# Loading v of the first batch once, in the layout of the later products, and turning eight units on TensorE in 128 by 32 tiles

## The chip, the cores and the metric

The kernel runs on one core of one Trainium2 chip. A core has five engines that matter here: TensorE (PE; its weight loads are listed as PEld), VectorE (DVE), ScalarE (ACT), GpSimd (POOL) and SyncE (SP), which here does nothing but issue DMAs. The metric is the device time of one execution in microseconds (us); a kernel's time is the median of its runs.

## What is computed

```python
# attention: q, k, v are (8 batches, 8 heads, 576 rows, 64), float32
scores = scale * np.matmul(q, k.transpose(0, 1, 3, 2))
thresh = np.max(scores, axis=-1, keepdims=True) - tau
scores = np.where(scores >= thresh, scores, -1000000000.0)
scores = scores - np.max(scores, axis=-1, keepdims=True)
attn = np.exp(scores)
attn = attn / (np.sum(attn, axis=-1, keepdims=True) + 1e-09)
attn_out = np.matmul(attn, v)
# rows: (batch, head, row, 64) -> x of 4608 x 512
# feed-forward: w_a, w_b are 512 x 1536, w_out 1536 x 512, given as float64
a = x @ w_a
b = x @ w_b
out = a * b @ w_out
```

## The kernel before

Heads are worked on in pairs: `pairs` holds 32 of them (8 batches, HP = 4 pairs each), and a tile's 128 partitions hold two heads of 64. A unit `(i, u)` is 128 query rows of pair i (u = 0 to 3), or the last 64 rows of two pairs together (u = NT). The main loop goes over the units, one slot g for each. Slot g computes the scores of unit g (line 404), their maximum (L411), the exponentials (L432) and the threshold with the sums (L435), and then has the weights of earlier units turned, so that the 576 keys lie on partitions, and multiplied by v (L546, output `pv`). Between these steps `advance` emits portions of the feed-forward block (L854, L750, L920 and L990), in amounts worked out when the program is built. `keep_order` fixes the order of the instructions on each engine to the order in which they are emitted.

The weights of a unit are turned in one of two ways.

- The first BY_PE = 8 units (u = 0 and 1 of the four pairs of the first batch) are turned by TensorE in `turn_pe`, one slot later. `diagonals` (L462) makes a diagonal matrix `dg` of the reciprocal sums; a matmul with 64 columns of the weights `tw` as the stationary operand and `dg` as the moving one (L483) gives these 64 keys by 128 rows, transposed and normalised, in PSUM. There are NSLOT = 9 slots of 64 keys and two heads j, so 18 such matmuls a unit, each in a 128 by 64 tile of the array. Two ScalarE copies (L485) and one VectorE copy (L486) take them to `wT`. `weighted_unit` multiplies by v one slot after that.
- All later units are turned by `normalise` (L454), a VectorE transpose of 32 by 32 blocks (L502) and a trip through DRAM: `turn_blocks` writes `swap`, `turn_back` reads it into `wT`.

The two ways leave the keys in different places. With TensorE, slot s and partition p (of 64) hold key 64 s + p. With the block transpose, partition c 32 + p and slot s hold a key of half c, block s, place p: 288 c + 32 s + p for the first batch. The rows of v have to lie in the same way in the tile `vm`, whose partitions are two heads of 64.

`load_v` therefore loads v of the first four pairs twice. The first load, from SyncE (L214), is two moves of 144 KB a pair in the layout of `turn_pe`. It is emitted ahead of the loop for pair 0, and at the end of slots 0, 1 and 2 for pairs 1 to 3. The second load, `again=True`, is four moves of 72 KB a pair in the layout of the block transpose, into the same tile. It is emitted at the end of slots 8 to 11 through `post`, which at that time issues at once on SyncE (L144). The products of units u = 2, 3 and NT of the first batch (L546 and L629) read what it brings.

In the same stretch of slots the float64 weights are brought in and turned into float32: 36 pieces, loaded by `load_weights` on SyncE (L271), at most one at each of five places of a slot, some of them held back until an instruction of TensorE has run. ScalarE (L298, L299), GpSimd (L305, L324) and VectorE (L311, L319) convert them, two or three pieces a slot.

SyncE issues its DMAs strictly in the order emitted. DMA number n of the queue waits, by the program's semaphores, for number n - 8.

Of the kernel before, what the change touches and what calls it, by code (L numbers as in the profile page):

```python
# [10 lines left out]
FP32 = mybir.dt.float32  # L11
# [12 lines left out]
BY_PE = 8  # L24
# [30 lines left out]
def kernel(  # L55
# [38 lines left out]
    nc = tc.nc  # L94
    B, H, S, D = q.shape
    P = 128
    Q = 32
    DM = H * D
    DFF = w_a.shape[1]
    HP = H // 2  # L100
    NT = 4
# [10 lines left out]
    NSLOT = 9  # L112
# [5 lines left out]
    def pool(name, bufs, **kw):  # L118
        return ctx.enter_context(tc.tile_pool(name=name, bufs=bufs, **kw))

    const = pool("const", 1)
    loads = pool("loads", 3)
# [5 lines left out]
    def banks(n, name):  # L128

        return psum.tile([P, 2, 512], FP32, tag="banks", name=name)[:, :, 0:n]  # L130
# [4 lines left out]
    loaded = {}  # L135
# [3 lines left out]
    def post(key, *moves):  # L139

        if not state["paced"]:
            for move in moves:
                state["turn"] += state["over"]
                (nc.scalar if state["turn"] % 2 else nc.sync).dma_start(*move)  # L144
        else:
            at = len(bulk)
            if key[0] in ("tw", "wT"):
                while at and bulk[at - 1][0][0] not in ("tw", "wT") and bulk[at - 1][1] >= state["slot"] - 1:
                    at -= 1
            bulk.insert(at, (key, state["slot"], moves))  # L150
# [47 lines left out]
            engine.dma_start(room[:, :, j * D:(j + 1) * D], rows.rearrange("(n p) d -> p n d", p=R))  # L198
        loaded.setdefault(i, {})[name] = room

    def load_v(i, again=False):
        b, hp = pairs[i]
        if not again:
            loaded[i]["v"] = loads.tile([P, NSLOT, D], FP32, tag="vm", bufs=HP, name="vm")
        for j in range(2):
            rows, half = v[b, 2 * hp + j], loaded[i]["v"][j * D:(j + 1) * D]
            if i >= HP or again:
                if i < HP:
                    rows = rows.rearrange("(c s p) d -> p c s d", c=2, p=Q)
                else:  # L210
                    rows = rows.rearrange("(p c s) d -> p c s d", c=2, p=Q)
                post(("v", i), *((half[c * Q:(c + 1) * Q], rows[:, c]) for c in range(2)))
            else:
                nc.sync.dma_start(half, rows.rearrange("(s p) d -> p s d", p=D))  # L214

# [8 lines left out]
    for f in range(NG):  # L226
        for c in range(HP):
            for dst, w in ((wa_sb, w_a), (wb_sb, w_b)):
                src = []
                for r in range(2):  # L230
                    chunks = [(2 * c + e) % HP * 2 + (r + (c >= HP // 2)) % 2 for e in range(2)]
                    cols = slice(f * CW + r * CH, f * CW + (r + 1) * CH)
                    rows = w[:, cols].bitcast(U32).rearrange("(k p) f -> p k f", p=D)
# [110 lines left out]
    load_rows(2, "k", rooms[5])  # L344
    load_weights(RAWS)
    load_v(0)
    load_rows(3, "q", rooms[6])
    load_rows(3, "k", rooms[7])
# [19 lines left out]
    def prep_pe(i, name):  # L368

        m = loaded[i][name]  # L370
        if name == "q":
            mT = first_sb[:, i * S:(i + 1) * S]
        else:
            mT = work.tile([P, S], FP32, tag="kT", bufs=HP, name="kT")
        tp = banks(SH, "tp")
        for c in range(2):
            for n in range(NR // 2):
                nc.tensor.transpose(tp[:, c, n * R:(n + 1) * R], m[:, c * (NR // 2) + n], ident[0:R, 0:R])
        prepared.setdefault(i, {})[name] = mT
        return mT, tp  # L380
# [86 lines left out]
    def turned_tile(here=None):  # L467
        if here == (0, NT):
            return sums_sb[:, NSUM - TURNED:].rearrange("p (g s e) -> p g s e", g=G + 1, s=NSLOT)
        return work.tile([P, G + 1, NSLOT, Q], FP32, tag="wT", bufs=2, name="wT")  # L470

    def turn_pe(i, u):

        ws, dg = weights.pop((i, u))
        ws = [w.rearrange("p n e -> p (n e)") for w in ws]
        wT = turned_tile()[:, 0:G].rearrange("p g s e -> p (g s e)").rearrange("p (s w) -> p s w", w=P)
        turned[i, u, "pe"] = [wT[:, :, y * D:(y + 1) * D] for y in range(2)]
        tp = banks(512, "tp").rearrange("p y (s q) -> p y s q", s=NT)
        last = banks(P, "tp")
        for s in range(NSLOT):  # L480
            for j, w in enumerate(ws):
                to = (last[:, 0] if s == 2 * NT else tp[:, s // NT, s % NT])[j * D:(j + 1) * D]
                nc.tensor.matmul(to, w[:, s * D:(s + 1) * D], dg[:, j], start=True, stop=True)  # L483
        for y in range(2):
            nc.scalar.copy(wT[:, y * NT:(y + 1) * NT], tp[:, y])  # L485
        nc.vector.tensor_copy(wT[:, 2 * NT], last[:, 0])  # L486
# [524 lines left out]
    def store(n):  # L1011

        for _ in range(n):
            post("out", pending.pop(0))
# [79 lines left out]
    kT, tp = prep_pe(0, "k")  # L1094
# [22 lines left out]
    for g in range(len(units) + PV_LAG):  # L1117
# [14 lines left out]
        if here:  # L1132
            i, u = units[g]
# [33 lines left out]
        if g < 3:  # L1167
            kT, tp = prep_pe(g + 1, "k")
            nc.scalar.copy(kT.rearrange("p (c k) -> p c k", c=2), tp)
        if 0 < g <= BY_PE:  # L1170
            turn_pe(*units[g - 1])
# [42 lines left out]
        for p in range(1, NPR):  # L1214
            if g == first[p] - 1:
                load_v(p)
        if BY_PE <= g < BY_PE + HP:
            load_v(g - BY_PE, again=True)
        store(written)
        if g > BY_PE:  # L1220
            if held:
# [60 lines left out]
```

## Time and profile before

| what | us |
|---|---|
| median of 3 runs | 1401.8 |
| the three runs | 1399.14, 1401.8, 1404.3 |
| the profiled execution, its own time | 1400.57 |
| its span on the core | 1398.8 |

| engine | busy us | share of the span |
|---|---|---|
| PE | 1361.5 | 97% |
| PEld | 1258.5 | 90% |
| DVE | 1013.9 | 72% |
| ACT | 680.8 | 49% |
| POOL | 492.8 | 35% |

The profile is one execution recorded by the hardware profiler. Busy time is an average over stages with different limits, so the first 200 us have to be looked at by themselves. A matmul of float32 leaves two records: the 144 turning instructions of L483 stand as 288. A tile given as 128*64 is a tile of the array with 128 rows and 64 columns. DMA issues appear as SPq; the time of such a line can contain the issue's own wait. The DMA share is the mean busy share of the 16 DMA engines; in the busiest stretches it reads above 1.

Lines that the change touches, from the groups and the tiles of the trace:

| line | what | count | one takes |
|---|---|---|---|
| L483 | PE, 128*64, 128 columns | 288 | 272 to 475 ns |
| L485 | ACT, `wT` from PSUM, 128x512 | 16 | 1.07 us for two |
| L214 | SPq, first load of v, 144 KB | 8 | 595 to 638 ns |
| L144 | SPq, second load of v, 72 KB | 16 | 447 to 1587 ns, median 453 |

### The profile page before, as it was taken

How to read it: one execution, taken by the hardware profiler on the slowest of the kernel's cores; microseconds unless marked ns; L12 is line 12 of the kernel's file. 1: busy time of each engine (PE TensorE's matmuls, PEld its weight loads, DVE VectorE, ACT ScalarE, POOL GpSimd, SP SyncE). 2: the span in 40 equal slices, each digit the busy share in tenths (PEclk: the TensorE clock that was granted, in tenths of full speed). 3: DMA queues.
4: the chain of work that ended last, by engine and by line, in shares of the span. 5: the costliest groups of instructions: out<-in, count | busy, mean ns of one | idle time of the engine just before them, and what ended most of it. 6: DMA issues, size and time to landing. Idle time of an engine off the chain costs nothing.

```text
span 1398.8 us, 76307 instructions
## 1 busy us (share of the span) xinstructions
PE 1361.5 (97%) x33836; PEld 1258.5 (90%) x33836; DVE 1013.9 (72%) x2205; ACT 680.8 (49%) x1248; POOL 492.8 (35%) x675
## 2 busy tenths in 40 slices
PE   7889999999999999999999999999999999999998
PEld 5677588999998799999999999998899998799998
DVE  6999877787777768786767776778777776745425
ACT  6977555545554555544454545454545455431110
POOL 2764543424150607060515142332515060708100
PEclk9999999999999999999999999999999999999999
DMA  9977876667666775676556775566656775550000
GB/s 211 241 212 223 204 206 173 174 170 187 174 154 168 190 192 155 176 190 160 143 143 160 186 180 159 136 190 169 181 130 161 199 190 154 137 146 19 4 19 18
DMA packets 327449, 223.21 MB, mean 160 GB/s; under 512 B 171600, under 2 KB 311632, under 8 KB 327120
## 3 DMA queue, kind: packets, MB, share of 16 engines
q1 hardware_dynamic: 323936, 216.95, 60.1%
q8 instruction: 266, 4.36, 1.3%
q10 hardware_dynamic: 3184, 1.38, 0.4%
q14 instruction: 63, 0.52, 0.1%
HBM read 128.58 MB, written 89.65 MB: 156 GB/s over the span
## 4 chain that ended last, share of the span: by engine, by line
PE 88%; DMA 5%; DVE 4%; SPq 2%; issue 1%; ACT 1%; ACTq 0%; DVEq 0%
PE pab L750 29%; PE po L920 22%; PE pab L854 18%; PE sc L404 9%; PE pv L546 9%; SPq L144 1%; DMA vm<-in_v_dram 1%; DMA wT<-swap 1%; DVE tw L435 1%; DVE mx L411 1%; DMA more_u<-in_moe_w_a_dram 1%; DVE low L311 0%; DMA more_u<-in_moe_w_b_dram 0%; DVE tw L502 0%; DMA sums_u<-in_k_dram 0%
## 5 line engine op out<-in xcount | busy, mean ns | idle before, releaser
L454 ACT ACTIVATE tw<-tw,rcp 128x576 f32<-128x576 f32 x272 | 196.1, 768 | 201.3 <-DVE rcp L448 201.3
L411 DVE TENSOR_REDUCE mx<-sc 128x1 f32<-128x576 f32 x288 | 204.6, 752 | 121.2 <-PE sc L404 120.9
L432 ACT ACTIVATE tw<-sc,bias,scalars 128x576 f32<-128x576 f32 x288 | 239.6, 832 | 10.4 <-DMA qT<-in_q_dram 0.4
L712 POOL TENSOR_TENSOR h<-h,u 128x512 f32<-128x512 f32 x28 | 35.2, 1277 | 590.4 <-DVE h L824 414.1
L435 DVE SCALAR_TENSOR_TENSOR tw<-sc,thr,tw 128x576 f32<-128x576 f32 x288 | 220.9, 797 | 12.3 <-ACT tw L432 11.9
L920 PE MATMUL po<-wo_sb,h 64*64 64x256 f32 (+1 forms) x3408 | 210.5, 367 | 0.0
L502 DVE STREAM_TRANSPOSE tw<-tw 128x576 f32<-128x576 f32 x272 | 194.4, 752 | 0.8 <-ACT tw L454 0.8
L920 PEld LDWEIGHTS po<-wo_sb,h 64*64 64x64 f32 x3408 | 169.8, 133 | 14.9
L404 PE MATMUL sc<-kT,qT 64*64 64x288 f32 x2016 | 170.3, 404 | 1.8 <-issue 0.9
L546 PE MATMUL pv<-wT,vm 64*64 64x128 f32 (+2 forms) x4896 | 164.0, 275 | 3.7 <-DMA vm<-in_v_dram 1.4
L546 PEld LDWEIGHTS pv<-wT,vm 64*64 64x64 f32 x4896 | 153.2, 133 | 12.0 <-issue 4.0
L920 PE MATMUL po<-sums_u,h 64*64 64x256 f32 x2448 | 156.6, 376 | 0.0
L883 POOL TENSOR_TENSOR h<-h 128x256 f32<-128x256 f32 x168 | 117.2, 731 | 110.9 <-PE po L920 106.1
L750 PE MATMUL pab<-xU,wb_sb 64*64 64x128 f32 x4352 | 137.8, 269 | 0.0
L920 PEld LDWEIGHTS po<-sums_u,h 64*64 64x64 f32 x2448 | 126.1, 133 | 12.3 <-DVE h L862 0.5
L750 PEld LDWEIGHTS pab<-xU,wb_sb 64*64 64x64 f32 x4352 | 133.3, 133 | 1.8 <-ACT h L806 0.5
L404 PEld LDWEIGHTS sc<-kT,qT 64*64 64x64 f32 x2016 | 108.8, 133 | 17.3 <-issue 4.9
L431 ACT ACTIVATE bias<-mx,scalars 128x1 f32<-128x1 f32 x288 | 82.7, 287 | 66.1 <-DVE mx L411 65.6
L553 ACT COPY xT<-pv 128x128 f32<-128x128 f32 (+1 forms) x68 | 17.6, 259 | 193.5 <-PE pv L546 193.5
L750 PE MATMUL pab<-xS,wa_sb 64*64 64x128 f32 x2176 | 108.5, 269 | 0.8 <-issue 0.8
L554 DVE COPY xT<-pv 64x128 f32<-64x128 f32 (+1 forms) x136 | 38.1, 280 | 80.5 <-PE pv L546 79.0
L535 ACT COPY kept<-po 128x512 f32<-128x512 f32 x65 | 34.8, 535 | 120.3 <-PE po L920 106.4
(163 smaller groups left out, 2468.7 us busy)
## 6 DMA issues: line engine op xcount, KB each, us to landing
wT<-swap SPq DMA_DIRECT2D x242, 288.0 KB, 3.8
swap<-tw SPq DMA_DIRECT2D x480, 144.0 KB, 3.1
vm<-in_v_dram SPq DMA_DIRECT2D x128, 72.0 KB, 2.6
swap<-tw SPq DMA_DIRECT2D x128, 72.0 KB, 2.9
kT<-in_k_dram SPq DMA_DIRECT2D x112, 72.0 KB, 3.2
wT<-swap SPq DMA_DIRECT2D x56, 144.0 KB, 3.6
out_dram<-kept SPq DMA_DIRECT2D x27, 256.0 KB, 3.7
qT<-in_q_dram SPq DMA_DIRECT2D x112, 40.0 KB, 2.8
```

The costliest lines, as they stand in the source:

```text
L404: nc.tensor.matmul(sc[m][o * D:o * D + wide, c], qT[r, q0:q0 + wide], kT[r, c * SH:(c + 1) * SH], start=True, stop=True)
L411: nc.vector.tensor_reduce(mx[:, c], sc[j], axis=AX.XY, op=ALU.max)
L431: nc.scalar.activation(bias[:, j:j + 1], mx[:, j:j + 1], AF.Copy, scale=e_nscale)
L432: nc.scalar.activation(wb[j], sb[j], AF.Exp, bias=bias[:, j:j + 1], scale=e_scale)
L435: nc.vector.scalar_tensor_tensor(out=wv, in0=sb[j], scalar=thr[:, j:j + 1], in1=wv, op0=ALU.is_ge, op1=ALU.mult, accum_out=sums[:, j:j + 1])
L454: nc.scalar.activation(w, w, AF.Copy, scale=rcp[:, j:j + 1])
L502: nc.vector.transpose(w, w)
L546: nc.tensor.matmul(pv[c * D:(c + 1) * D, y], vm[rows, s], wT[y](rows, s), start=(s == 0), stop=(s == NSLOT - 1))
L750: nc.tensor.matmul(out[c * D:(c + 1) * D, r, f * P:(f + 1) * P], w[g][k][rows, w0:w0 + D], moving[k][rows], start=(fresh and k == 0 and f ...
L854: nc.tensor.matmul(pab[c:c + columns(), r], w[rows, f // n, k, fs + c:fs + c + columns()], moving, start=(k == 0), stop=(k == H - 1))
L883: (nc.vector if state["over"] else nc.gpsimd).tensor_tensor(*a, **kw)
L920: nc.tensor.matmul(po[c * D:(c + 1) * D, r, y, cut], ht[rows, t0:t0 + D], other[rows, f, cut], start=(f == 0), stop=(f == NF // 2 - 1))
```

## The change

v of the first batch is loaded once, in the layout that only the second load had: four moves of 72 KB a pair from SyncE, at the places of the first load. The second load goes. To fit, `turn_pe` puts keys of both halves c into each slot: instead of 64 neighbouring columns of the weights it takes two groups of 32, one from each half of the 576 keys, each by a matmul of its own whose output goes to 32 partitions. A unit has 36 such matmuls in 128 by 32 tiles instead of 18 in 128 by 64 tiles, each with the same 128 moving columns. The copies out of PSUM and the order of all other instructions stay as they were.

```diff
-    def load_v(i, again=False):
+    def load_v(i):
         b, hp = pairs[i]
-        if not again:
-            loaded[i]["v"] = loads.tile([P, NSLOT, D], FP32, tag="vm", bufs=HP, name="vm")
+        loaded[i]["v"] = loads.tile([P, NSLOT, D], FP32, tag="vm", bufs=HP, name="vm")
         for j in range(2):
             rows, half = v[b, 2 * hp + j], loaded[i]["v"][j * D:(j + 1) * D]
-            if i >= HP or again:
-                if i < HP:
-                    rows = rows.rearrange("(c s p) d -> p c s d", c=2, p=Q)
-                else:
-                    rows = rows.rearrange("(p c s) d -> p c s d", c=2, p=Q)
-                post(("v", i), *((half[c * Q:(c + 1) * Q], rows[:, c]) for c in range(2)))
+            if i < HP:
+                rows = rows.rearrange("(c s p) d -> p c s d", c=2, p=Q)
             else:
-                nc.sync.dma_start(half, rows.rearrange("(s p) d -> p s d", p=D))
+                rows = rows.rearrange("(p c s) d -> p c s d", c=2, p=Q)
+            moves = [(half[c * Q:(c + 1) * Q], rows[:, c]) for c in range(2)]
+            if i < HP:
+                for move in moves:
+                    nc.sync.dma_start(*move)
+            else:
+                post(("v", i), *moves)
...
         for s in range(NSLOT):
-            for j, w in enumerate(ws):
-                to = (last[:, 0] if s == 2 * NT else tp[:, s // NT, s % NT])[j * D:(j + 1) * D]
-                nc.tensor.matmul(to, w[:, s * D:(s + 1) * D], dg[:, j], start=True, stop=True)
+            for c in range(2):
+                for j, w in enumerate(ws):
+                    at = j * D + c * Q
+                    to = (last[:, 0] if s == 2 * NT else tp[:, s // NT, s % NT])[at:at + Q]
+                    k0 = (c * NSLOT + s) * Q
+                    nc.tensor.matmul(to, w[:, k0:k0 + Q], dg[:, j], start=True, stop=True)
...
-        if BY_PE <= g < BY_PE + HP:
-            load_v(g - BY_PE, again=True)
```

## The prediction

> **What bounds the kernel now.** I read the page's first part, then busy time by stage, then the chain of waits, then the TensorE and SyncE timelines of the stages that the edit touches.
>
> The columns of the first fence are: stretch and its length, then for PE, PEld, DVE, ACT and POOL the busy time (instructions), granted clock, DMA share, GB/s.
>
> ```profile
> 20.00:40.00 20.00, 17.30 (x326) 14.05 (x326) 17.02 (x44) 16.27 (x35) 11.40 (x15) 1.00 1.17 222
> 40.00:85.00 45.00, 36.48 (x796) 32.31 (x786) 42.34 (x90) 38.81 (x80) 34.86 (x41) 0.96 0.88 215
> 85.00:125.00 40.00, 35.41 (x583) 31.93 (x577) 39.21 (x85) 31.72 (x64) 22.27 (x23) 1.00 0.87 253
> 125.00:200.00 75.00, 72.31 (x1165) 51.95 (x1165) 66.91 (x144) 44.71 (x84) 39.77 (x30) 1.00 0.80 204
> 200.00:1398.00 1198.00, 1187.62 (x30943) 1118.78 (x30934) 839.14 (x1824) 539.17 (x970) 382.02 (x559) 1.00 0.57 150
> ```
>
> There are three regimes. Until 40 us the 16 DMA engines are full (share 1.17). From 40 to 125 us VectorE is the bound: it is busy 42.34 of 45 and 39.21 of 40 us, while TensorE has idle time (8.5 and 4.6 us). From 200 us TensorE is busy 99% and sets the end. Everything that the change touches lies before 125 us, so it can reach the end only by moving the moment at which that first part is through. The amount of work that TensorE does inside it is fixed by the emitted order.
>
> The chain of waits, by line, names two things that the change removes or alters:
>
> ```profile
> PE pab L750 29%; PE po L920 22%; PE pab L854 18%; PE sc L404 9%; PE pv L546 9%; SPq L144 1%; DMA vm<-in_v_dram 1%; DMA wT<-swap 1%; DVE tw L435 1%; DVE mx L411 1%; DMA more_u<-in_moe_w_a_dram 1%; DVE low L311 0%; DMA more_u<-in_moe_w_b_dram 0%; DVE tw L502 0%; DMA sums_u<-in_k_dram 0%
> ```
>
> The vm share (about 14 us) looks large. In order of time the chain's longest vm step is 8.52 us at 30.77, one of the first loads waiting in a full queue; the steps of the second load are 3.14 and 2.86 us at 92 and 102 us, and VectorE worked without a gap beside both.
>
> The TensorE timeline shows one turn of today's form (line 483), the product that waits for v behind it, and a later product of 128 columns; idle time and its cause stand in brackets.
>
> ```profile
> 27.89 2.19 PE L483 MATMUL tp<-first_u,tw 128*64 128x128 f32 x36
> 30.00 1.53 PE L404 MATMUL sc<-kT,first_u 64*128 64x288 f32 x8
> 31.98 0.33 PE L546 MATMUL pv<-wT,vm 64*64 64x64 f32 x4 [0.45 <-DMA vm<-in_v_dram]
> 32.87 1.26 PE L546 MATMUL pv<-wT,vm 64*64 64x64 f32 x68 [0.56 <-DMA vm<-in_v_dram]
> ...
> 113.27 2.20 PE L546 MATMUL pv<-wT,vm 64*64 64x128 f32 x72
> ```
>
> A unit's 18 turning instructions leave 36 records ("passes"). 36 passes in 2.19 us, less the last one's own length (0.27), is 1.92, or 53.3 ns a pass. A single pass lasts 273 ns, so several overlap. That two column halves run side by side, 107 ns of streaming each, is the reading that also fits the product: its 72 passes of 128 columns over four 64x64 tiles take 2.20 us, 107/4 = 27 ns each.
>
> **The change part by part.**
>
> *Turning in 128x32 tiles.* 18 instructions a unit become 36, so 72 passes of 128 columns each, for eight units; the two ScalarE copies and the VectorE copy behind them do not change, nor does the last slot's wait for its bank. No row has a 128x32 tile. Lower bound: four tiles of 107 ns side by side give 72 x 26.7 = 1.92 us, as today; a gain is excluded, because each quarter of the array still streams 128 columns 18 times. Upper bounds: two at a time, 72 x 53.3 = 3.84 us (+1.92 a unit, +15.4 in all); one at a time, 72 x 107 = 7.7 us (+5.8 a unit, +46 in all). The nearest row is the product of four 64x64 tiles, 72 passes in 2.20 us against 2.19 now. Today's two column halves already stream different data side by side at no loss, so I take 0.
>
> The Trainium skill ("TensorE: Matmul & The Clock Gate", section "Measured speedup vs the span model") speaks against taking the full overlap: three column tiles of 32 ran 2.38 times as fast as one after the other, and no four of them stand there. By that rule, as an estimate, a pass would cost 107/2.38 = 45 ns and a unit 3.2 us, +10.5 us of TensorE time in all, which is still below the 11.2 us of idle time worked out under the rivals. No run so far shows such a tile.
>
> *First load of v.* Two moves of 144 KB a pair become four of 72 KB, same bytes, same rows of 256 B. On SyncE the 144 KB move takes 0.606 us (median of 8) and the 72 KB one 0.45 (median of the 16 reloads): 4 x 0.45 - 2 x 0.606 = +0.6 us a pair, +2.4 us for four. Behind them in SyncE's queue stand the rows of pair 3 (first case) and then the weight pieces. The work that hides this is the DMA backlog: these moves land 7 to 8 us after issue, with the DMA share above 1, so a later issue meets a shorter queue. If the cover failed it would be the whole 2.4 us. Each move also waits for the eighth before it, so four small ones among eight leave 4 x 72 + 4 x 256 = 1.3 MB in flight, 6 us at 222 GB/s, still no gap. What may show is v itself: the product already waits 1.4 us for it, three times, and the fourth move ends 0.6 us later. I take +0.5; bounds 0 and 2.4.
>
> *Reload removed.* Sixteen moves of 72 KB go, and with them their time on SyncE:
>
> ```profile
> 83.32 3.08 SPq L144 DMA_DIRECT2D vm<-in_v_dram  x4
> 86.56 0.35 SPq L271 DMA_DIRECT2D more_u<-in_moe_w_out_dram  x1
> ...
> 90.93 3.19 SPq L144 DMA_DIRECT2D vm<-in_v_dram  x4
> 94.17 0.97 SPq L144 DMA_DIRECT2D wT<-swap  x2
> ...
> 101.06 1.94 SPq L144 DMA_DIRECT2D vm<-in_v_dram  x4
> ...
> 112.27 1.95 SPq L144 DMA_DIRECT2D vm<-in_v_dram  x4
> ```
>
> That is 10.2 us of SyncE and 1.18 MB (4.7 us at 253 GB/s). Queued behind them are w_out pieces and reads of swap. No product waits for the reload: the two that follow it, at 113 and 120 us, start with no idle time before them. VectorE has 0.8 us of idle time in the whole stretch, so w_out pieces that come sooner are converted no sooner. Bounds: 0 and, if all idle time of TensorE from 85 to 200 us (4.6 + 2.7) were owed to this queue, -7.3. I take -0.4, half of VectorE's idle time.
>
> *Sum*: 0 + 0.5 - 0.4 = +0.1 us on the profiled execution's 1400.6 (span 1398.8, 1.8 around it). The median shown is 1401.8, 1.2 above it; on that median the forecast is 1402, no change. What a measurement can tell from no change is about 0.5%, 7 us: below 1394.8 is faster, above 1408.8 slower.
>
> **Rivals.**
>
> *Column tiles one after the other (slower).* Place: TensorE, eight turns between 18 and 77 us. Idle time of TensorE that can swallow it: 2.7 + 8.5 = 11.2 us from 20 to 85. One at a time costs 46 - 11 = +35 us, 1437. It passes +7 when eight times (72s - 1.92) exceeds 18, that is from a spacing s of 58 ns a pass. Two at a time (53 ns) therefore costs only +4, 1406. The cover is uneven, which makes it dearer: the turn at 58.44 ended at 60.68 and VectorE took its result at 61.24, and the scores at 63.39 ended 0.2 us before VectorE needed them. Against: today's halves overlap without loss. For: no row has four full-height streams.
>
> *Second load was the brake (faster).* If SyncE's 10.2 us did hold the w_out pieces and swap reads, the end comes up to 7.3 us earlier, 1395. For: the chain names vm and SyncE. Against: VectorE's 39.21 of 40, and the absent idle time before the products.
>
> *The clock (either sign).* From 75 to 85 us the granted clock is 0.83, after TensorE idled 1.45 us before 78.36; the two groups after it took 2.08 and 1.81 us where others take 1.16 and 1.09, and VectorE then waited 1.43 us for scores. Denser turning could avoid this (-1.6) or longer waits add another such stretch (+1.6): 1400 or 1404.
>
> **How the numbers follow.** No change, including two at a time and the clock: 0.54, of which two tiles at a time 0.12. Slower: 0.32, namely one at a time or nearly 0.15, between 58 and 80 ns a pass, or two at a time where the uneven cover fails, 0.12, first loads that starve the weight pieces in the DMA-bound part 0.05. Faster: 0.14, the brake together with the clock. The predicted time is that of the likeliest case, 1402, whose own range is 1398 to 1406. The range goes down to 1395 for the brake and up to 1418: two at a time at full price with no cover, 1401.8 + 15.4. The serial case, 1437, lies outside it.
>
> **What would show it.** Turning line: 72 records in about 2.2 us a unit if I am right, 3.8 or 7.7 if not. First v moves: landing within 1 us of before, idle time of the product for vm at most 3 us. From 85 to 125 us: SyncE 10 us emptier, VectorE again about 98% busy; if its work there ends over 3 us sooner, the reload was the brake. From 200 us on both traces should agree. A granted clock that differs from 18 to 85 us, or a weight piece waited for where none was, would make the prediction wrong.

## The result, and the profile after

| | median us | runs | lowest to highest |
|---|---|---|---|
| before | 1403.01 | 17 | 1397.06 to 1405.34 |
| after | 1408.27 | 17 | 1402.62 to 1414.54 |

The ratio is 1.0038, with a 95% interval from 1.0023 to 1.0053: the changed kernel is 5.3 us slower. That is less than the 7 us set as "no change" beforehand, but the interval leaves out 1. The profiled execution took 1410.14 us, its span 1408.3.

Busy time by stage of the kernel after, up to 125 us, with the same columns as in the prediction:

```profile
20.00:40.00 20.00, 15.50 (x359) 12.23 (x348) 15.69 (x41) 14.72 (x31) 10.26 (x14) 0.91 1.12 217
40.00:85.00 45.00, 33.52 (x902) 29.25 (x902) 38.33 (x88) 36.34 (x78) 31.73 (x38) 0.96 0.87 213
85.00:125.00 40.00, 36.09 (x629) 32.51 (x629) 39.26 (x79) 31.69 (x62) 24.56 (x26) 1.00 0.71 212
```

The row from 40 to 85 us holds most of the news. VectorE, the bound of that stage, is busy 38.33 us where it was 42.34: 4.0 us less work done in the same time. TensorE has 106 more records there and yet is busy 3 us less. From 85 to 125 us VectorE is as full as before (39.26 against 39.21) while the DMA share fell from 0.87 to 0.71: the reload is gone, and nothing sped up for it. The row from 20 to 40 us is behind as well: VectorE did 15.69 us of work instead of 17.02, and the granted clock was 0.91 instead of 1.00.

The chain of waits of the kernel after, by engine and by line:

```profile
PE 89%; DVE 4%; DMA 3%; SPq 1%; issue 1%; ACT 1%; ACTq 0%; DVEq 0%
PE pab L754 29%; PE po L924 22%; PE pab L858 18%; PE sc L405 10%; PE pv L550 9%; DMA wT<-swap 1%; DMA sums_u<-in_k_dram 1%; SPq L144 1%; PE tp L487 1%; DVE mx L412 1%; DVE low L312 1%; DVE tw L436 1%; DMA raw<-in_moe_w_b_dram 0%; DVE tw L506 0%; DMA swap<-tw 0%
```

The vm share is gone (`vm` is the tile of v). "issue" is time in which an engine waited for nothing that the profile shows. Where it sits in the start-up, TensorE's timeline of the kernel after shows (start, length, and the idle time before in brackets):

```profile
18.72 2.17 PE L487 MATMUL tp<-first_u,tw 128*32 128x128 f32 x72 [0.55 <-DVE first_u L384]
...
48.41 1.61 PE L487 MATMUL tp<-first_u,tw 128*32 128x128 f32 x49
52.68 0.86 PE L487 MATMUL tp<-first_u,tw 128*32 128x128 f32 x23 [2.66 <-issue]
...
57.42 0.93 PE L550 MATMUL pv<-wT,vm 64*64 64x64 f32 x48
61.21 0.58 PE L550 MATMUL pv<-wT,vm 64*64 64x64 f32 x24 [2.86 <-issue]
62.45 3.72 PE L487 MATMUL tp<-first_u,tw 128*32 128x128 f32 x72 [0.67 <-DVE xT L558]
```

The first line answers the question that the prediction thought decisive: 72 passes take 2.17 us, so four 128 by 32 tiles run side by side without loss. A loss is in the two pairs that start at 48.41 and 57.42. A turn stops after 49 of its 72 records and a product after 48 of 72, for 2.66 and 2.86 us, in the middle of work whose operands were all there; no semaphore is named. The turn behind the second gap then runs at a lowered clock, 0.57 granted from 62.4 to 66.2 us, and takes 3.72 us instead of 2.17. The turn at 28.31, which is not shown, also takes 3.72 us (0.56 granted), with no such gap before it. In the profile of before no such gap stands ahead of 130 us.

The two gaps end 127 records apart. Between them, busy time of the kernel after:

```profile
52.50:61.10 8.60, 5.67 (x127) 4.95 (x126) 5.16 (x12) 5.34 (x11) 5.17 (x6) 1.00 1.07 249
```

In the trace, the instruction behind the second gap comes exactly 256 instructions of TensorE after the one behind the first: 127 matmul records, 126 weight loads and 3 waits for semaphores. That is one packet of the queue which brings TensorE its instructions; the page of the profile of the kernel after counts them (packets, MB, share):

```profile
q8 instruction: 269, 4.41, 1.3%
```

4.41 MB in 269 packets is 16.4 KB each; 269 x 256 is 68,864, and PE and PEld have 68,248 records together, 68,824 with TensorE's semaphore instructions. Before, there were 266 packets and 4.36 MB. In the trace, packets of this queue start at 49.88 and 58.37 us and take 1.31 and 1.28 us; each gap ends 1.5 us after its packet. So TensorE had run out of instructions, twice, at a time when the DMA engines were full of weight pieces (share 1.07). A weight piece takes about 8 us from issue to landing between 48 and 62 us.

How the time accumulates: VectorE's instruction that takes the thresholds of unit 12 starts at 111.97 us before and at 116.30 after, +4.3. Not all of this comes from the two gaps. At unit 4, ahead of both, the difference is already 1.6 us, behind waits for rows of q and k and the slow turn at 28.31. At unit 6, behind the first gap, it is still 1.65, where before TensorE waited for VectorE (1.57 us ahead of 50.99). At unit 7, behind the second gap and the slow turn at 62.45, it is 5.3. After unit 12 the difference goes to 6.1 us at unit 24, back to 3.6 near unit 70 and up to 10.2 at the end, 3.2 of that in one step at unit 129.

### The profile page after: what moved, and what is told of

It reads as the page before. It is cut to its first block, busy times and chain, and to the rows that moved or that the text cites. A ratio compares the mean times of both kernels' runs of the same rounds, so it can differ in the third digit from the quotient of the medians.

```text
span 1408.3 us, 76883 instructions
## 1 busy us (share of the span) xinstructions
PE 1362.3 (97%) x34124; PEld 1270.4 (90%) x34124; DVE 1014.3 (72%) x2205; ACT 679.8 (48%) x1248; POOL 492.5 (35%) x675
## 3 DMA queue, kind: packets, MB, share of 16 engines
q8 instruction: 269, 4.41, 1.3%
## 4 chain that ended last, share of the span: by engine, by line
PE 89%; DVE 4%; DMA 3%; SPq 1%; issue 1%; ACT 1%; ACTq 0%; DVEq 0%
PE pab L754 29%; PE po L924 22%; PE pab L858 18%; PE sc L405 10%; PE pv L550 9%; DMA wT<-swap 1%; DMA sums_u<-in_k_dram 1%; SPq L144 1%; PE tp L487 1%; DVE mx L412 1%; DVE low L312 1%; DVE tw L436 1%; DMA raw<-in_moe_w_b_dram 0%; DVE tw L506 0%; DMA swap<-tw 0%
## 5 line engine op out<-in xcount | busy, mean ns | idle before, releaser
L436 DVE SCALAR_TENSOR_TENSOR tw<-sc,thr,tw 128x576 f32<-128x576 f32 x288 | 220.9, 797 | 11.5 <-ACT tw L433 11.3
L924 PEld LDWEIGHTS po<-wo_sb,h 64*64 64x64 f32 x3408 | 174.5, 133 | 10.5
L405 PE MATMUL sc<-kT,qT 64*64 64x288 f32 x2016 | 173.7, 406 | 4.2 <-DVE xt L558 2.8
L924 PEld LDWEIGHTS po<-sums_u,h 64*64 64x64 f32 x2448 | 129.5, 133 | 8.6
L754 PE MATMUL pab<-xT,wa_sb 64*64 64x128 f32 x1856 | 93.1, 270 | 0.5 <-issue 0.4
```

What stands on the lines that cost most here:

```text
L405: nc.tensor.matmul(sc[m][o * D:o * D + wide, c], qT[r, q0:q0 + wide], kT[r, c * SH:(c + 1) * SH], start=True, stop=True)
L436: nc.vector.scalar_tensor_tensor(out=wv, in0=sb[j], scalar=thr[:, j:j + 1], in1=wv, op0=ALU.is_ge, op1=ALU.mult, accum_out=sums[:, j:j + 1])
L754: nc.tensor.matmul(out[c * D:(c + 1) * D, r, f * P:(f + 1) * P], w[g][k][rows, w0:w0 + D], moving[k][rows], start=(fresh and k == 0 and f ...
L924: nc.tensor.matmul(po[c * D:(c + 1) * D, r, y, cut], ht[rows, t0:t0 + D], other[rows, f, cut], start=(f == 0), stop=(f == NF // 2 - 1))
```

## The experiments

All ratios are to the kernel before, run on the same chip in between. Its medians there were 1408.74 us beside tiles_only, load_only, after_again and halves, 1409.17 beside late_split, after_due, after_diag and before_diag, and 1409.92 beside some_halves and after_diag_again.

### Which of the two edits

**tiles_only** has the new loop of `turn_pe` and leaves both loads of v as they were. It leaves out the order of v that would match, so the first eight units pair keys with other rows of v; the amount of work is the same.

> The turn in 128x32 tiles alone; v of the first batch is loaded twice as before (the products of the first eight units then pair wrong keys with v, the amount of work is the same). Theory A, the instruction supply of TensorE (36 instead of 18 instructions a unit while the DMA engines are full): +4 to +6 us on before, with idle stretches of 2 to 3 us that the trace puts to issue between 40 and 65 us. Theory B, the 32-column tile form itself (its passes or the clock): also +4 to +6 us, but with the turning passes spread out or at half clock and no such gaps. Theory C, the first load of v in small moves: 0 +- 1 us.

Measured: 1415.44 us, ratio 1.0048 [1.0028, 1.0069], +6.7 us. The stalls are there, on other instructions than in the kernel after:

```profile
40.56 0.93 PE L549 MATMUL pv<-wT,vm 64*64 64x64 f32 x49 [1.26 <-issue]
47.19 0.64 PE L404 MATMUL sc<-kT,first_u 64*128 64x288 f32 x2 [1.65 <-issue]
54.18 0.85 PE L486 MATMUL tp<-first_u,tw 128*32 128x128 f32 x19 [1.88 <-issue]
```

A stall in a product and in a score matmul, neither of which was edited, is not a matter of how the turning tiles lie in the array. Here the gaps do make the delay: the difference from the first profile of before is 0.15 us at unit 4 and 4.8 at unit 6.

**load_only** has the new load and none of the reload, with the old loop of `turn_pe`.

> v loaded once in four small moves a pair and no second load; the turn stays in 128x64 tiles of 18 instructions (the first eight units then pair wrong keys with v, the amount of work is the same). Theory A: 0 to -2 us on before, no issue gaps. Theory B: 0 to -2 us. Theory C: +4 to +6 us.

Measured: 1409.74 us, 1.0007 [0.9987, 1.0027], +1.0 us. The two load edits together are worth nothing that could be told apart from zero. Its profile has two short gaps of this kind (0.19 us at 62.20 and 0.94 at 68.89) although the number of matmuls is that of before, and it stands 2.6 us behind the first profile of before at unit 12.

**after_again** is the changed kernel once more, beside these.

> The changed kernel on the chip of the three others: +4 to +7 us on before. By theory A a second profile shows the gaps again, one packet of instructions (about 128 matmul records) apart, though not at the same length.

Measured: 1413.29 us, 1.0025 [1.0001, 1.0049]. Its two gaps fall on the same records as in the first profile, 23 and 24 records before the end of their groups:

```profile
51.81 1.50 PE L487 MATMUL tp<-first_u,tw 128*32 128x128 f32 x23 [3.55 <-issue]
60.61 0.58 PE L550 MATMUL pv<-wT,vm 64*64 64x64 f32 x24 [1.76 <-issue]
```

The place follows the count of instructions, the length does not.

### Tiles or number of instructions

**halves** keeps everything of the kernel before, also its 128 by 64 tiles, and cuts each turning matmul into two of 64 moving columns. It streams the same columns with as many instructions as the changed kernel.

```diff
-            for j, w in enumerate(ws):
-                to = (last[:, 0] if s == 2 * NT else tp[:, s // NT, s % NT])[j * D:(j + 1) * D]
-                nc.tensor.matmul(to, w[:, s * D:(s + 1) * D], dg[:, j], start=True, stop=True)
+            for n in range(2):
+                for j, w in enumerate(ws):
+                    to = (last[:, 0] if s == 2 * NT else tp[:, s // NT, s % NT])[j * D:(j + 1) * D, n * D:(n + 1) * D]
+                    nc.tensor.matmul(to, w[:, s * D:(s + 1) * D], dg[:, j, n * D:(n + 1) * D], start=True, stop=True)
```

> Before, with each turning matmul cut into two of 64 moving columns in the same 128x64 tile: 36 instructions a unit as after the change, the same streaming time, loads as before. Theory A: +3 to +6 us on before with issue gaps of 2 to 3 us, as it goes by the number of instructions. Theory B: 0 +- 1 us. Theory C: 0 +- 1 us.

Measured: 1415.75 us, 1.0048 [1.0027, 1.0069], +7.0 us: the whole loss without a single 128 by 32 tile and without an edit to the loads. TensorE's timeline of this kernel, and then its busy time between the gaps:

```profile
41.12 0.93 PE L547 MATMUL pv<-wT,vm 64*64 64x64 f32 x49 [1.45 <-issue]
...
48.04 0.64 PE L404 MATMUL sc<-kT,first_u 64*128 64x288 f32 x2 [1.95 <-issue]
...
55.87 0.80 PE L484 MATMUL tp<-first_u,tw 128*64 128x64 f32 x19 [2.86 <-issue]
```

```profile
34.00:41.00 7.00, 5.39 (x127) 4.40 (x127) 6.18 (x15) 6.05 (x13) 4.35 (x5) 1.00 1.13 220
41.00:48.00 7.00, 4.76 (x127) 4.12 (x127) 6.40 (x16) 5.82 (x13) 4.72 (x7) 1.00 1.12 235
48.00:55.80 7.80, 4.97 (x127) 4.38 (x127) 4.49 (x12) 3.60 (x8) 4.12 (x6) 0.78 1.07 242
```

Again 127 and 127 a block, with two waits for semaphores 256, whatever the instructions are. The difference from the first profile of before is 0.5 us at unit 4 and 6.4 at unit 6. The gaps in the profile of tiles_only fall on the same records (49, 2 and 19 left of their groups): equal counts, equal places.

**some_halves** does this in the five even slots alone, 80 matmuls more instead of 144 (`wide = 2 * D if s % 2 else D` as the moving columns).

> Before with the turning matmuls of five of the nine slots cut in two (80 additional TensorE instructions in the first eight units instead of 144). If the supply of instruction blocks is the limit: blocks of 127 matmul records still come 7 to 8 us apart while the DMA engines are full, so the delay at the twelfth unit is between none and that of the full cut (5 us), about +2 to +4 us, and the time +2 to +5 us. If the whole cut costs by a threshold that only the full count passes: 0 +- 1 us.

Measured: 1412.86 us, 1.0030 [1.0007, 1.0052], +2.9 us. In amount this fits a line with 144 matmuls (+4.6 to +7.0), but the interval, 1.0 to 7.3 us, is wide. Its profile has only 0.16, 0.58 and 0.81 us of such gaps in the start-up and stands 1.4 us behind the first profile of before at unit 12, so its place was not shown.

### Is it the full DMA engines alone

**late_split** adds the same 144 matmuls where the DMA engines are not full (share 0.67 from 330 to 484 us): it cuts the score matmuls of units 40 to 57 into two of 144 columns.

```diff
-            nc.tensor.matmul(sc[m][o * D:o * D + wide, c], qT[r, q0:q0 + wide],
-                             kT[r, c * SH:(c + 1) * SH], start=True, stop=True)
+            parts_of = 2 if 40 <= units.index((i, u)) < 58 else 1
+            for n in range(parts_of):
+                k0, k1 = n * SH // parts_of, (n + 1) * SH // parts_of
+                nc.tensor.matmul(sc[m][o * D:o * D + wide, c, k0:k1], qT[r, q0:q0 + wide],
+                                 kT[r, c * SH + k0:c * SH + k1], start=True, stop=True)
```

> Before, with each score matmul of units 40 to 57 cut into two of 144 columns: the same 144 additional TensorE instructions as the change makes, the same streaming time, but in a stretch where the DMA engines are two thirds busy. Theory A in its full form (the blocks of instructions queue behind the data, so the count matters only while the DMA engines are full): 0 +- 1.5 us on before, no issue gap over 1 us there. Rival A2 (144 instructions cost the same wherever they stand): +5 to +7 us.

Measured: 1414.75 us, 1.0037 [1.0019, 1.0055], +5.6 us. That the added matmuls cost nothing where the DMA engines are not full is refuted. Its start-up is that of before (112.51 us at unit 12, no gap), but the edited stretch is longer: from the thresholds of unit 39 to those of unit 57 it takes 153.6 us against 148.9. In the profiles of kernels without this edit the same stretch takes 148.3 to 151.9. Waits from 125 to 1400 us of this kernel (sum, number, longest), and then those of before:

```profile
PE pab L753 <- issue: 4.3, 9, 0.9
...
PE sc L407 <- issue: 2.3, 3, 0.9
...
PE pv L549 <- issue: 1.6, 4, 0.7
```

```profile
PE pab L750 <- issue: 3.6, 8, 1.0
...
PE pv L546 <- issue: 1.1, 2, 0.7
PE sc L404 <- issue: 0.9, 1, 0.9
```

The kernel before has these gaps too in its later part, 5.6 us in the three lines; with the added matmuls it is 8.2. But the second profile of before (before_again, below) has 8.9 us of them there, so these sums show no effect of the edit. There TensorE is the bound, and 127 passes at 27 ns use up a block in 3.5 us. Inside the edited stretch, steps of over 0.3 us from one pass to the next add up to 3.9 us instead of 0.5, where the kernels without this edit have 0 to 2.0; the score passes take 19.6 us instead of 16.9 (one gap of 1.07 among them). So against the first profile of before some 3.4 us are gaps and some 1.7 us the passes' own cost, a pass of half the columns taking 32.3 ns where half of 58.7 would be 29.3. The split between the two rests on one profile of each. That second part has no counterpart in the turning of the changed kernel (2.17 us against 2.19).

### Does a shorter DMA queue help

**after_due** is the changed kernel with the weight pieces due one slot later (`n <= g + 1` for `n <= g + 2`), meant to leave fewer of them ahead of the instructions.

> The changed kernel with weight pieces asked for one slot ahead instead of two, so that fewer bytes lie ahead of a block of instructions in the DMA engines. Theory A: the issue gaps between 40 and 65 us shrink to under 1 us and the time falls to before +0 to +2, unless weight pieces now come late (then ScalarE waits for them and the time stays or rises). Rival A2: the gaps stay, +4 to +7 us.

Measured: 1409.7 us, 1.0007 [0.9989, 1.0025]. The time is that of before, but the profile does not show why:

```profile
51.61 1.40 PE L487 MATMUL tp<-first_u,tw 128*32 128x128 f32 x23 [3.22 <-issue]
...
59.31 0.58 PE L550 MATMUL pv<-wT,vm 64*64 64x64 f32 x24 [0.43 <-issue]
...
65.82 0.27 PE L858 MATMUL pab<-xT,wa_sb 64*128 64x128 f32 x1 [1.05 <-issue]
```

The first gap is as long as ever, the second nearly gone, and there are two others, of 0.51 us at 31.35 and of 1.05. They add up to 5.2 us, against 5.5 in the first profile of the changed kernel, and unit 12 comes at 115.29. But the profiled execution took 1416.14 us, the second longest of twelve whose median is 1409.7, so the profile does not stand for the timed executions. From 16 to 60 us the pieces landed 5.4 to 7.3 us after issue (medians by kind) instead of 5.8 to 7.4, so the edit shortened the queue little. Inconclusive on the mechanism.

### Taking instructions away

**after_diag** takes 144 matmuls out of the changed kernel elsewhere in the same stretch. The early products multiply both heads of a slot in one matmul each of 128 columns, in diagonal 64 by 64 tiles, 18 instead of 36 a unit; one ScalarE copy stands in place of three copies. **before_diag** does the same to the kernel before.

```diff
...
-        pv = product([lambda rows, s, t=t: t[rows, s] for t in wT], loaded[i]["v"], P)
+        pv = banks(P, "pv")[:, 0]
+        for s in range(NSLOT):
+            for j in range(2):
+                rows = slice(j * D, (j + 1) * D)
+                nc.tensor.matmul(pv[rows], loaded[i]["v"][rows, s], wT[rows, s], start=(s == 0), stop=(s == NSLOT - 1))
...
-        settle(x_of[b, 0][:, hp, u * P:(u + 1) * P], pv, 0, D, ([], []))
+        nc.scalar.copy(x_of[b, 0][:, hp, u * P:(u + 1) * P], pv)
```

> The changed kernel with the early products of v in one matmul of 128 columns for each head and slot (diagonal 64x64 tiles) instead of two of 64: 18 instructions a unit less, so the count of TensorE is again that of before; 0.96 us more streaming a unit, and one copy out of PSUM instead of three (two VectorE copies of 0.23 us less a unit). Theory A: no issue gap over 1 us; -5 to +1 us on before. Rival A2: the same. Rival B2 (what costs is the denser burst of the turn itself, 72 records in 2 us, not the total): gaps of 2 to 3 us remain, +2 to +6 us.

> Before with the same product of 128 columns: 144 instructions less than before and 16 VectorE copies less. Theory A: -2 to -7 us on before, and less than the gain of the same edit on the changed kernel, since before's instructions came in time. Without the instruction supply, the VectorE copies alone: 0 to -4 us, and the same gain on both kernels.

Measured: after_diag 1407.63 us, 0.9991 [0.9973, 1.0009]; before_diag 1410.26 us, 1.0008 [0.9991, 1.0025]. With as many matmuls as before, the changed kernel is as fast as before: unit 12 at 111.51 us, and no gap of TensorE for instructions ahead of 125 us. With 144 fewer than before, nothing is gained. The edit also makes an early product longer (2.18 us instead of 1.28) and takes away copies, which could hide a gain; but this is the same in both kernels. A fixed price per instruction would make the edit worth as much on before as on after, and it took off some 6 us there (from +4.6 and +5.3 in other rounds to -1.5) and added 1.1 us here [-1.3, +3.5]. So the price is not fixed: in this stretch the kernel before sits near where the supply just suffices.

**after_diag_again** repeats it on another chip.

> The changed kernel with the early products in one matmul of 128 columns, a second time: -3 to +1 us on before.

Measured: 1410.34 us, 1.0003 [0.9982, 1.0024]. The same, and no version here beats the kernel before by more than the error.

**before_again** is one more profile of the kernel before.

> The kernel before, profiled on the chip of the other runs, to compare traces on one chip: no idle stretch over 1 us that is put to issue before 130 us; the slots before 130 us at the same times as in the first profile within 1 us.

Its start-up does have gaps:

```profile
61.40 0.49 PE L483 MATMUL tp<-first_u,tw 128*64 128x128 f32 x5 [0.69 <-issue]
...
69.69 0.48 PE L546 MATMUL pv<-wT,vm 64*64 64x64 f32 x5 [2.66 <-issue]
```

Before runs short as well, by 2.66 us in this execution, and was 3.3 us later at unit 12 than in the first one. Neither profile is typical by itself: this execution took 1414.2 us, 4.3 above the median on that chip. The first profile of before, set beside that of the changed kernel, would overstate what the gaps cost, which is why the timed comparisons carry the verdict.

## Why the prediction was right or wrong

The time lies in the range (1395 to 1418) and within 0.5%, as forecast. But the sum said +0.1 us and the runs say +5.3 [+3.2, +7.4], so a term was mis-sized, and the runs show which. The time is also above the 1398 to 1406 given to the likeliest case: it lies in the range only by the room left for two tiles at a time without cover, which did not happen. That part of the hit is luck.

- **Turning in 128x32 tiles, "I take 0".** This is the step that failed. Its reading of the array was right: 72 records in 2.17 us a unit. What it priced was the streaming alone. The 18 instructions more a unit, 144 in all, were costed at nothing beside it; halves shows that they alone, in the old tiles, cost 7.0 us [3.8, 9.7]. The gaps in its start-up are TensorE waiting for its own instructions, of which the prediction has no term.
- **First load of v, +0.5.** It is within the error: load_only, which holds both load edits (+0.5 and -0.4 in the sum), gives +1.0 [-1.8, +3.8]. The four moves of a pair took 2.08 to 3.09 us on SyncE (1.8 foreseen). The product's wait for v did not grow: it vanished in the first profile of after and was 0.6 us in after_again. The transposing matmuls of pair 3 (L379) waited 2.14 and 1.32 us for its rows at 25.62 and 27.63, where the first profile of before has a wait of 0.88 us. tiles_only, with the old loads, waits 2.28 us for the k rows at the same place, and late_split stands there 2.90 us; so such waits come without the new loads too, and what the loads add to them is inside the error of load_only.
- **Reload removed, -0.4.** The place was as forecast: SyncE is empty of it, no product had waited for it, VectorE is as full as before. Sign and size are lost in the error of load_only.
- **Second load was the brake.** Dead by the same lines: 4.7 us of transfer went, and VectorE did 39.26 us of work in 40, after 39.21. load_only, at -1.8 us or above, leaves no room for -7.3.
- **Column tiles one after the other.** Dead by the first line of the timeline. The slower side came all the same, by another mechanism. This rival had the place right, TensorE between 18 and 77 us with VectorE waiting behind it; the mechanism was wrong.
- **The clock.** The turn at 62.45 is 1.55 us longer at the lowered clock, the size that the rival gave, and stands right behind a gap for instructions. The turn at 28.31 is as much longer, behind waits for rows of q and k. So the clock did differ between 18 and 85 us, which the prediction named as a sign against itself. Before's slow groups at 78.36 are absent.
- **"From 200 us on both traces should agree".** They do not quite: the difference is 6.1 us at about 200 us, falls to 3.6 and ends at 10.2. But the two profiles of before differ by more than that (11.5 us at unit 143), so single traces can't tell this apart.

That instructions come in blocks of 256, and that the places of the gaps follow from the number of instructions, is shown by kernels as different as after, tiles_only and halves. The thirteen traces say more. In each, counted in TensorE's instructions, the packets of this queue can be matched with the blocks that they bring. All 22 gaps put to issue ahead of 135 us fall on the first instruction of a block, which starts 1.3 to 1.7 us after its packet ended. For the 210 packets from the 31st on, a packet starts 0.6 to 1.0 us (medians of the traces) after TensorE entered the block before; at the 22 gaps it started 2.2 to 6.0 us after that, 3.84 and 5.69 in the first profile of after. So a block seems to be asked for when TensorE enters the one before it, and the late ones came late because their packets started late. That these stood behind weight pieces is a reading: it fits the DMA share above 1, but no run tested it directly; after_due was meant to, and hardly moved the queue.

How long a block lasts decides whether that matters. Before, it was 127 / 796 x 45 = 7.2 us between 40 and 85 us, after 127 / 902 x 45 = 6.3, gaps included. In the first profile of after the gaps end 6.6 and 8.5 us after TensorE entered the block before (at 46.04 and 52.68). In the first profile of before, the block that starts at 65.71 does so 1.33 us after its packet ended, without a gap: the kernel before is right at the edge, as before_again and before_diag also say. What the rest of the loss after unit 12 consists of, and whether the loads give back the 2 us between after_again and tiles_only, stays open. A turn of both groups of 32 columns with one instruction was not tried.

## What to carry to other kernels

Cutting matmuls into smaller tiles that run side by side costs no streaming time, but it doubles the instructions, and TensorE can run out of them: here 144 more matmuls of float32 (576 instructions) cost some 5 to 7 us, in a kernel that was near the edge already, with hardly any more streaming. Count the instructions of a stage, not only its columns; a group that stops in the middle with "issue" as the releaser, at equal distances in records, is what a late block of instructions looks like. Look for a place nearby to save as many: with 144 taken out of the products the loss was gone. And profile the unchanged kernel more than once: the gaps of before added up to 0 us in one profile and to 3.4 in the other, those of the changed kernel to 5.5 and 5.3.

## What the hardware showed that was not expected

- TensorE's instructions arrive in blocks of 256, over the same DMA engines as data, and a late block stopped TensorE for up to 3.6 us while these were full (after_again), for up to 1.1 us later on (after). The Trainium skill ("Runtime: NRT & Kernel Launch", section "Instruction fetch mechanics") has the blocks of 256 and a fetch of the next during the current; on that the trace agrees. It calls the cost of crossing a block "mostly hidden". That holds for most blocks here (after block 30, at most 12 of 210 in a trace start behind a gap of over 0.2 us), but not in the start-up.
- A matmul of float32 is four instructions of TensorE (two records and two weight loads), so a block is only some 64 of them.
- Four 128 by 32 tiles overlap in full: 2.17 us for 72 passes of 128 columns. The estimate of 3.2 us that the prediction worked out from three tiles in the Trainium skill ("TensorE: Matmul & The Clock Gate", section "Measured speedup vs the span model") does not hold for these four.
